# Order of the work in the last stage: first cast of g, w_out in half blocks, banks emptied ahead of g

## Chip, cores and metric

One core of one Trainium2 chip. The metric is the device time of one execution in microseconds (us); a time is the median of several executions.

## The reference

Sliding-window attention with four sink positions, a soft mixture of experts, and a feed-forward block, all in float32. The change lies in the last of the three:

```
x = attention(q, k, v)                     # (3072, 512)
c = softmax(x @ phi, over the slots)       # (3072, 32)
x = c @ slot_out                           # slot_out: (32, 512)
h = x @ w_in                               # (3072, 2048)
g = h - tanh(h)
out = g @ w_out                            # (2048, 512)
```

The host passes `w_out` (and `w_in`) as float64 in 64-bit words; the kernel makes float32 of it itself.

## The kernel before

Every engine's instructions stand in the order in which the program writes them; there is no scheduler. The last stage begins some 235 us into the span. As x is c times a matrix of 32 rows, `x @ w_in` is done as c times (slot_out @ w_in): the "small weights" `W`, 32 rows per 512 columns, are computed by `w_mm` into three PSUM banks (`acc[3]`, `cv_t`, `acc[2]`), and their rows are written to the tiles `w_st[x]` as a high and a low part: `rows_a(x)` casts on ScalarE, `rows_b(x)` subtracts on VectorE (and copies on GpSimd for x = 2). The rest of W goes the same way through `whs_part(x)` (ScalarE) and `wls_part(x)` (VectorE) into `whs` and `wls`, from which `rows4` copies rows later, in steps 5, 11 and 20.

Then come 96 steps. A step s belongs to a chunk c of 512 tokens and to a block f of 128 of the 2048 columns of h. Its parts stand in several steps of the program:

- `hmm(s)` on TensorE: one matmul makes h for chunk and block; it is issued at the end of step s-1.
- `act_y(s)` on ScalarE: tanh of a scaled h in place (L1184), its square into u (L1185). `dve_part(s)` on VectorE: g = u * h (L1204).
- `split(s)`, issued in step s+1: ScalarE casts g to `gh` (L1191), GpSimd subtracts, `gl = g - gh` (L1192).
- `omm(s)`, issued in step s+3: twelve matmuls add gh*whi, gh*wlo and gl*whi to four PSUM banks `acc[0..3]` (tiles o0 to o3; t counts the banks, one for each 128 tokens). In the last step of a group of blocks the three matmuls of a bank stand together, so that bank 0 is done first.
- `evac(s)`, behind the last step of a group: the four banks are copied to SBUF, or added to what is there; after block 15 SyncE issues the output's DMA, one of 128x512 for each bank.

The first chunks don't go through all 16 blocks at once, since `w_out` isn't ready: the groups (chunk, first block, end) are

```python
groups = [(0, 0, 2), (1, 0, 4), (0, 2, 6), (1, 4, 10), (0, 6, 12), (1, 10, 16), (0, 12, 16)] + [(c, 0, 16) for c in range(2, NT // CK)]
```

so `evac` runs in steps 3, 8, 12, 18, 24, 30, 34 and then every 16. Step 4 is the one step without `omm`: it has `hmm(5)` alone.

Ahead of its first use a block f of `w_out` is converted from 64 to 32 bits: `pre_conv` has four VectorE instructions of 128x512, "1" (L108), "2" (L113), "3" (L118), "g" (L127), and a square "s" on ScalarE (L122). Then `wsplit(f)` on GpSimd makes `whi` (L1032) and `wlo` (L1033), and `wload(f + 6)` has SyncE fetch a later block. A block takes two steps: "1" and "2" in the step with ph = 0, "3", "g", `wsplit` and `wload` in the next. `dve_part` puts g behind the first of the VectorE instructions that it is given as `fills`. With `CO = 2`, block f is ready in step 2f-1; `omm` reads block 9 first in step 18 and block 15 first in step 30.

Of the kernel before, what the change touches and what calls it, by code (L numbers as in the profile page):

```python
# [51 lines left out]
WACT = ()  # L52
DL, S0 = 2, 9
CK = 512
CO = 2
SPL = 2
DRAIN = "slota:mi trans slotb av3 av2 av1 d13 d14 d15 pst:sc lg2:sc lg3:sc sink:mi x0:sc,sc max pre exp slots x1:pT,av0 t0 t1 cmax:sc x2:sc,sc trd:sc x3:pT,av0 t2 t3 ext:sc trl:sc csum:sc s00:sc s01 slotc s02 acc0 s10:mi s11 acc1 sT:av0"
XENG = "AAAA"
# [79 lines left out]
def tile_kernel(ctx: ExitStack, tc: tile.TileContext, qk, vv, v0, v0t, nw, phi, w1, w2,  # L138
# [17 lines left out]
    def run(ctx, fast):  # L156
# [30 lines left out]
        for i in range(NR):  # L187
            pool, n = raw_p if i in RAW else ring2 if i in FREE else ring1, 1024 if i in HALF else 2048
# [28 lines left out]
        def ring_t(i, lo, n):  # L217
            if i == NR:
                return xt_t[lo // 512][:, lo % 512:lo % 512 + n]
            if i == NR + 1:  # L220
                return x2[0][:, lo:lo + n]
            return sv(order[i if i < NR else i - NR - 2], lo, n)
# [683 lines left out]
        def raw_of(f):  # L906
            return wraw[(f - 1) % 6]

        def wload(f):
            SP.dma_start(raw_of(f), w_out[P * f:P * f + P, :])  # L910
# [98 lines left out]
        def pre_conv(f, ops):  # L1009
            if f not in pcv:  # L1010
                wf[f] = wf_b[f % 3]
                pcv[f] = conv.start(raw_of(f), wf[f], cv_t if f > 1 else None)
            fns = {"1": conv.v1, "2": conv.v2, "3": conv.v3, "s": conv.sq, "g": conv.guard_dve,
                   "i": conv.ge_pool, "m": conv.mul_pool}
            for o in ops:
                fns[o](pcv[f])
# [10 lines left out]
        def wsplit(f):  # L1027
            hi, lo = whl[f]
            if f in WACT:
                ACT.copy(hi, wf[f])  # L1030
            else:
                POOL.tensor_scalar(hi, wf[f], 1.0, 0.0, op0=ALU.mult, op1=ALU.add)  # L1032
            POOL.tensor_tensor(lo, wf[f], hi.bitcast(F32), op=ALU.subtract)  # L1033
# [15 lines left out]
        for r in range(2):  # L1049
# [17 lines left out]
            for f in range(8):  # L1067
                for g in range(4):
                    t = ring_t(16 + 8 * r + 4 * (f // 4) + g, 512 * (f % 4), 512)
                    PE.matmul(yo[NS * g:NS * g + NS, :], hT[:, f, NS * g:NS * g + NS],  # L1070
                              t, start=f == 0, stop=f == 7)
# [13 lines left out]
            for x in range(2):  # L1085
# [3 lines left out]
                o = 16 * r  # L1089
# [10 lines left out]
        def w_of(f):  # L1100
            x, o = (f, 0) if f < 2 else (2, f - 2) if f < 4 else (2 + f // 4, f % 4)
            return w_st[x][:, P * o:P * o + P]
# [8 lines left out]
        def rows_a(x):  # L1111
            for g in range(2 if x < 2 else 1):
                ACT.copy(w_st[x][NS * g:NS * g + NS, :], W[x][0:NS, :])

        def rows_b(x):
            w = w_st[x]
            hi = w.bitcast(F32)[0:NS, :]
            if x > 1:
                POOL.tensor_scalar(w[NS:2 * NS, :], hi, 1.0, 0.0, op0=ALU.mult, op1=ALU.add)
            DVE.tensor_tensor(w[2 * NS:G3, :], W[x][0:NS, :], hi, op=ALU.subtract)  # L1120
# [3 lines left out]
        steps = [(c, f, f == lo, f == hi - 1) for c, lo, hi in groups for f in range(lo, hi)]  # L1124
        N = len(steps)

        def h_of(s):
            return h_b[s % 2]

        def hmm(s):  # L1130
            c, f = steps[s][:2]
            PE.matmul(h_of(s), w_of(f), cT[0:G3, CK * c:CK * c + CK], start=True, stop=True)  # L1132
# [27 lines left out]
        def whs_part(x):  # L1160
            ACT.copy(whs[:, w_lo[x]:w_lo[x] + w_n[x]], W[x])

        def wls_part(x):
            c = slice(w_lo[x], w_lo[x] + w_n[x])
            DVE.tensor_tensor(wls[:, c], W[x], whs.bitcast(F32)[:, c], op=ALU.subtract)
# [15 lines left out]
        def act_y(s, small=True):  # L1181
            h = h_of(s)
            if small:
                ACT.activation(h, h, AF.Tanh, scale=ca)  # L1184
                ACT.activation(u_b[s % 3], h, AF.Square, scale=cc ** 0.5)  # L1185
            else:
                ACT.activation(u_b[s % 3], h, AF.Square)

        def split(s):
            g, gh, gl = g_b[s % 3], gh_b[s % NG], gl_b[s % NG]  # L1190
            ACT.copy(gh, g)  # L1191
            POOL.tensor_tensor(gl, g, gh.bitcast(F32), op=ALU.subtract)  # L1192

        def dve_part(s, small, fills):
            h, u, g = h_of(s), u_b[s % 3], g_b[s % 3]
            fills = list(fills)

            def fill():
                if fills:
                    fills.pop(0)()  # L1200

            fill()
            if small:
                DVE.tensor_tensor(g, u, h, op=ALU.mult)  # L1204
                fill()
            else:
                DVE.tensor_scalar(mk, u, TB * TB, None, op0=ALU.is_gt)
                DVE.tensor_scalar(z, u, TB * TB, None, op0=ALU.min)
                DVE.tensor_scalar(u, z, cg[6], None, op0=ALU.mult)
                for q in (5, 4, 3, 2, 1, 0):  # L1210
                    DVE.scalar_tensor_tensor(u, u, cg[q], z, op0=ALU.add, op1=ALU.mult)
                fill()
                DVE.tensor_tensor(g, u, h, op=ALU.mult)
                ACT.activation(z, h, AF.Tanh)
                DVE.tensor_tensor(z, h, z, op=ALU.subtract)
                DVE.copy_predicated(g, mk, z)
            while fills:
                fill()

        def omm(s, hi=True, lo=True, ts=range(4)):  # L1220
            c, f, first, last = steps[s]
            gh, gl = gh_b[s % NG], gl_b[s % NG]
            wh, wl = whl[f]

            def mm(t, a, w, start, stop):
                PE.matmul(acc[t], a[:, P * t:P * t + P], w, start=start, stop=stop)  # L1226

            for t in ts:
                if hi:
                    mm(t, gh, wh, first, False)  # L1230
                    mm(t, gh, wl, False, False)
                if last and lo:
                    mm(t, gl, wh, False, True)
            if lo and not last:
                for t in ts:
                    mm(t, gl, wh, False, False)
# [2 lines left out]

        def evac(s):  # L1240
            c, f = steps[s][:2]
            for t in range(4):
                sp = sp_b[c % 2][t]
                if c > 1 or (c, f) in ((0, 1), (1, 3)):
                    if t % 2:
                        DVE.tensor_copy(sp, acc[t])
                    else:
                        ACT.copy(sp, acc[t])
                elif t % 2:
                    ACT.copy(tmp[t], acc[t])  # L1250
                    POOL.tensor_tensor(sp, sp, tmp[t], op=ALU.add)
                else:
                    DVE.tensor_tensor(sp, acc[t], sp, op=ALU.add)
                if f == 15:
                    r0 = CK * c + P * t
                    SP.dma_start(out[r0:r0 + P, :], sp)

        f2 = keep.tile([1, 1], F32, name="f2")
        fmx = h_of(N)[0:1, 0:P]
# [6 lines left out]
        def x_wmax():  # L1266
            ACT.activation(z, whs, AF.Square)
            DVE.tensor_reduce(wmax, z, axis=AX.X, op=ALU.max)
# [3 lines left out]
        def step(s, small, pre=False):  # L1272
            o = s - (DL + 1)
            if pre and s < 5:
                o = 1 if s == 3 else -1
            if o >= 0:
                omm(o)
            if 1 < s + 1 < N:
                hmm(s + 1)
            if fast and s == N:  # L1280
                PE.transpose(fmx, wmax, ident)
            f, ph = divmod(s + CO, 2)
            todo = 2 <= f < 16 and (pre or s >= S0)
            fills = []
            if todo:
                fills = [lambda p=p: pre_conv(f, p) for p in ("3g" if ph else "12")]
            if s < N:
                act_y(s, small)
            if 0 <= s - 1 < N:
                split(s - 1)  # L1290
            if todo and ph == 0:
                pre_conv(f, "s")
            if fast and s == N:
                x_flag()
            if s < N:
                dve_part(s, small, fills)
            if todo and ph:
                wsplit(f)
                if f + 6 < 16:
                    wload(f + 6)  # L1300
            if (pre or s >= S0) and s in row_at:
                rows4(row_at[s])
            if o >= 0 and steps[o][3]:
                evac(o)
            if fast and s == 40:
                x_wmax()

        act_y(0)
        rows_a(1)
# [3 lines left out]
        fq = ctx.enter_context(tc.tile_pool(name="fq", bufs=1))  # L1313
        w_split_tiles(fq, range(NB, 16))
        dve_part(0, True, (lambda: None, lambda: rows_b(1)))
        rows_a(2)
        hmm(1)
        act_y(1)
        split(0)
        rows_b(2)  # L1320
        for x in range(3):
            whs_part(x)
        omm(0, lo=False, ts=(0, 1))
        dve_part(1, True, (lambda: None, lambda: [wls_part(x) for x in range(3)]))
        hmm(2)
        omm(0, lo=False, ts=(2, 3))
        omm(0, hi=False)
# [99 lines left out]
```

## Time and profile before

| | us |
|---|---|
| median of 3 executions | 545.78 (544.48 to 547.65) |
| the profiled execution | 544.87 |
| its span in the trace | 543.1 |
| TensorE busy in the span | 510.2 (94%) |
| mean granted clock of TensorE | 0.993 |

The span is what the trace covers; 1.8 us of the profiled execution lie around it. TensorE is busy nearly all the time, so what matters in the last stage is when it isn't, and at what clock it runs. A matmul lasts longer than the distance to the next one, since they are pipelined: distances between starts are what counts.

### The profile page before, as it was taken

The numbers are of one execution on the slowest core, as the hardware profiler recorded it, in microseconds if no ns is written. First come the engines' busy times: TensorE is split into PE (matmuls) and PEld (weight loads), VectorE is DVE, ScalarE is ACT, GpSimd is POOL, SyncE is SP. The second block draws the span as 40 slices with busy tenths as digits, with TensorE's granted clock in tenths as the row PEclk, the third lists the DMA queues.
The fourth block names the chain that finished last, engine by engine and source line by source line (L and its number), as shares of the span: only waits on it lengthen the run. The fifth ranks groups of instructions, "written<-read, shape, count | busy, mean of one in ns | idle before, by whom it ended". The sixth has DMA issues, their size and how long they took to land.

```text
span 543.1 us, 10098 instructions
## 1 busy us (share of the span) xinstructions
PE 510.2 (94%) x3650; PEld 357.3 (66%) x3650; DVE 314.8 (58%) x672; ACT 356.0 (66%) x1020; POOL 264.4 (49%) x289
## 2 busy tenths in 40 slices
PE   8898999989989998889998998999999999999996
PEld 4555555555555532248776876888888888888884
DVE  2999998998787487667876773322232232223221
ACT  4899898898896333449776765665656565556550
POOL 0566755656734000047897896644343434444441
PEclk9999999999999999999999998999999999999999
DMA  8979886433467899962321002200020020002002
GB/s 307 410 284 346 321 313 226 128 102 121 160 235 248 301 361 410 409 240 77 116 80 40 0 1 77 78 2 0 1 78 1 0 78 0 1 0 78 1 1 82
DMA packets 21993, 77.59 MB, mean 143 GB/s; under 512 B 2866, under 2 KB 4018, under 8 KB 20018
## 3 DMA queue, kind: packets, MB, share of 16 engines
q1 hardware_dynamic: 21938, 76.89, 38.7%
q8 instruction: 30, 0.49, 0.4%
q14 instruction: 25, 0.20, 0.1%
HBM read 70.59 MB, written 6.29 MB: 142 GB/s over the span
## 4 chain that ended last, share of the span: by engine, by line
PE 64%; DVE 12%; DMA 11%; ACT 7%; POOL 3%; issue 2%; SPq 1%; POOLq 0%; DVEq 0%; ACTq 0%
PE o L1226 48%; DMA w<-in_w 7%; PE h L1132 4%; PE av L655 3%; ACT w L591 3%; DVE mx L582 3%; DMA w<-in_qk 2%; DVE w L637 2%; PE sc L561 2%; DMA w<-in_vv 1%; PE mi L427 1%; DVE w L576 1%; PE pT L623 1%; ACT w L575 1%; DVE w L635 1%
## 5 line engine op out<-in xcount | busy, mean ns | idle before, releaser
L1192 POOL TENSOR_TENSOR gl<-g,gh 128x512 fp32r<-128x512 f32 x96 | 123.7, 1290 | 121.3 <-ACT gh L1191 120.4
L1204 DVE TENSOR_TENSOR g<-u,h 128x512 f32<-128x512 f32 x96 | 66.0, 688 | 165.6 <-ACT u L1185 164.9
L1226 PE MATMUL o<-whi,gh 128*128 128x512 f32 x384 | 153.2, 399 | 4.2 <-issue 1.9
L1226 PE MATMUL o<-wlo,gh 128*128 128x512 f32 x384 | 152.5, 397 | 1.7 <-POOL wlo L1033 1.7
L1184 ACT ACTIVATE h<-h 128x512 f32<-128x512 f32 x96 | 55.9, 582 | 98.4 <-PE h L1132 98.2
L1226 PE MATMUL o<-whi,gl 128*128 128x512 f32 x384 | 109.2, 392 | 0.0
L1226 PEld LDWEIGHTS o<-whi,gh 128*128 128x128 f32 x384 | 73.0, 190 | 22.7 <-POOL whi L1032 2.4
L1226 PEld LDWEIGHTS o<-wlo,gh 128*128 128x128 f32 x384 | 73.1, 190 | 19.2 <-POOL wlo L1033 2.3
L1226 PEld LDWEIGHTS o<-whi,gl 128*128 128x128 f32 x384 | 72.7, 189 | 16.3 <-POOL gl L1192 0.6
L601 POOL TENSOR_TENSOR w<-w,su 128x528 f32<-128x528 f32 x38 | 41.3, 1086 | 53.6 <-DVE su L598 34.8
L591 ACT ACTIVATE w<-w,nb 128x132 f32<-128x132 f32 x152 | 59.6, 393 | 1.2
L1185 ACT ACTIVATE u<-h 128x512 f32<-128x512 f32 x96 | 57.3, 597 | 3.0
L1191 ACT CAST gh<-g 128x512 fp32r<-128x512 f32 x96 | 58.9, 614 | 0.4 <-DVE g L1204 0.3
L655 PE MATMUL av<-w,w 128*64 128x256 f32 (+1 forms) x448 | 48.3, 344 | 0.0
L561 PE MATMUL sc<-w 64*64 64x200 f32 (+2 forms) x768 | 45.3, 332 | 1.8 <-DMA w<-in_qk 0.9
L1032 POOL TENSOR_SCALAR whi<-wf 128x512 fp32r<-128x512 f32 x16 | 10.2, 639 | 62.0 <-DMA w<-in_w_out 59.1
L1132 PE MATMUL h<-cT,wst 96*128 96x512 f32 x96 | 38.0, 398 | 0.6 <-DVE wst L1120 0.5
L561 PEld LDWEIGHTS sc<-w 64*64 64x64 f32 x768 | 26.5, 133 | 15.1 <-issue 10.1
L655 PEld LDWEIGHTS av<-w,w 128*64 128x64 f32 x448 | 25.8, 136 | 15.3 <-issue 9.2
L637 DVE TENSOR_TENSOR w<-pT,c_t 128x512 f32<-128x512 f32 x46 | 31.2, 679 | 0.0
L623 PE MATMUL pT<-c_t,w 128*128 128x128 f32 x148 | 23.6, 282 | 6.3 <-POOL w L601 3.8
L591 ACT ACTIVATION_READ_ACCUMULATOR w<-w,nb 128x1 f32 x152 | 28.3, 187 | 0.0
(252 smaller groups left out, 707.7 us busy)
## 6 DMA issues: line engine op xcount, KB each, us to landing
w<-in_w SPq DMA_DIRECT2D x32, 512.0 KB, 10.2
w<-in_w SPq DMA_DIRECT2D x14, 1024.0 KB, 6.7
w<-in_qk SPq DMA_DIRECT2D x16, 780.0 KB, 6.7
w<-in_w_out SPq DMA_DIRECT2D x15, 512.0 KB, 3.6
w<-in_vv SPq DMA_DIRECT2D x16, 384.0 KB, 4.2
w<-in_w_in SPq DMA_DIRECT2D x8, 512.0 KB, 4.8
out<-xt SPq DMA_DIRECT2D x12, 256.0 KB, 2.2
win_t<-in_w_in SPq DMA_DIRECT2D x4, 512.0 KB, 9.6
```

Source lines behind the costliest of these rows:

```text
L561: PE.matmul(sc_t[i][u][w, o:o + n], a[r, 64 * j:64 * j + 64], kslc(a, lo, n)[r, :], start=True, stop=True)
L591: ACT.activation(Z[:, u, :], Z[:, u, :], AF.Exp, bias=nb[:, u:u + 1], scale=SCALE, accum_out=su[:, u, :])
L601: (POOL if i < NQ - 1 else DVE).tensor_tensor(Z, Z, su.to_broadcast([P, 4, CH]), op=ALU.mult)
L637: DVE.tensor_tensor(d[:, :, 0, :], src, mL, op=ALU.mult)
L655: PE.matmul(dst[r, :], v[:, t, r], l, start=start, stop=stop, skip_group_check=True)
L1132: PE.matmul(h_of(s), w_of(f), cT[0:G3, CK * c:CK * c + CK], start=True, stop=True)
L1184: ACT.activation(h, h, AF.Tanh, scale=ca)
L1185: ACT.activation(u_b[s % 3], h, AF.Square, scale=cc ** 0.5)
L1191: ACT.copy(gh, g)
L1192: POOL.tensor_tensor(gl, g, gh.bitcast(F32), op=ALU.subtract)
L1204: DVE.tensor_tensor(g, u, h, op=ALU.mult)
L1226: PE.matmul(acc[t], a[:, P * t:P * t + P], w, start=start, stop=stop)
```

## The change

It has four parts. At the start of the stage the first cast of g (`split(0)`) moves ahead of `hmm(1)`, of tanh and square of step 1 and of the small weights' rows; `whs_part` and `wls_part` move up behind it, `rows_a(2)` behind step 1's tanh and square, and `rows_b(2)` behind step 1's g. A table `plan` gives the half blocks that a step converts: one in two steps of three and two in the third, from step 3 on. `evac` is called ahead of g: its ScalarE copies stand in front of the conversion's square, and its VectorE work is returned as the first `fills` of the step. With that the output's DMAs of a chunk are issued bank 0, bank 2, bank 1, bank 3 (for the chunk whose banks are added up: 1, 3, 0, 2).

```diff
-CO = 2
@@ evac
-            for t in range(4):
+            fresh = c > 1 or (c, f) in ((0, 1), (1, 3))
+
+            def one(t):
                 sp = sp_b[c % 2][t]
-                if c > 1 or (c, f) in ((0, 1), (1, 3)):
+                if fresh:
...
+            dve = [t for t in range(4) if t % 2 == fresh]
+            for t in range(4):
+                if t not in dve:
+                    one(t)
+            return [lambda t=t: one(t) for t in dve]
@@ step
-            f, ph = divmod(s + CO, 2)
-            todo = 2 <= f < 16 and (pre or s >= S0)
+            todo = plan.get(s, ()) if pre or s >= S0 else ()
...
+            if o >= 0 and steps[o][3]:
+                fills += evac(o)
+            for f, ph in todo:
+                fills += [lambda f=f, p=p: pre_conv(f, p) for p in ("3g" if ph else "12")]
+                if not ph:
+                    pre_conv(f, "s")
...
-            if o >= 0 and steps[o][3]:
-                evac(o)
...
+        turns = [(2, 1)] + [(f, ph) for f in range(3, 16) for ph in range(2)]
+        plan, s_ = {}, 3
+        while turns:
+            n = 2 if s_ % 3 == 1 else 1
+            plan[s_], turns = turns[:n], turns[n:]
+            s_ += 1
@@ ahead of the steps
         dve_part(0, True, (lambda: None, lambda: rows_b(1)))
+        split(0)
+        hmm(1)
+        for x in (0, 2, 1):
+            whs_part(x)
+            wls_part(x)
+        act_y(1)
         rows_a(2)
-        hmm(1)
-        act_y(1)
-        split(0)
-        rows_b(2)
-        for x in range(3):
-            whs_part(x)
         omm(0, lo=False, ts=(0, 1))
-        dve_part(1, True, (lambda: None, lambda: [wls_part(x) for x in range(3)]))
+        dve_part(1, True, (lambda: None, lambda: rows_b(2)))
         hmm(2)
         omm(0, lo=False, ts=(2, 3))
```

Lines below L57 have a number smaller by one in the changed kernel, and by other amounts below `evac`. The first place is ScalarE at the start of the stage. Before, the rows from the casts of the small weights to the third tanh (h is tanh in place, u the square, gh the cast of g, whs the rest of the small weights) are:

```order
L1113 CAST wst1_3234<-cvt_2878 32x128 x2
L1113 CAST wst2_3235<-o2_2875 32x256
L1184 ACTIVATE h1_2872<-h1_2872 128x512
L1185 ACTIVATE u1_3299<-h1_2872 128x512
L1191 CAST gh0_3301<-g0_3295 128x512
L1161 CAST whs_3293<-o3_2876 128x128
L1161 CAST whs_3293<-cvt_2878 128x128
L1161 CAST whs_3293<-o2_2875 128x256
L1184 ACTIVATE h0_2871<-h0_2871 128x512
```

In the changed kernel the same stretch is:

```order
L1112 CAST wst1_3234<-cvt_2878 32x128 x2
L1190 CAST gh0_3301<-g0_3295 128x512
L1160 CAST whs_3293<-o3_2876 128x128
L1160 CAST whs_3293<-o2_2875 128x256
L1160 CAST whs_3293<-cvt_2878 128x128
L1183 ACTIVATE h1_2872<-h1_2872 128x512
L1184 ACTIVATE u1_3299<-h1_2872 128x512
L1112 CAST wst2_3235<-o2_2875 32x256
L1183 ACTIVATE h0_2871<-h0_2871 128x512
```

The cast of g moved up over the cast into wst2 and step 1's tanh and square, the three casts into whs went with it, and the cast into wst2, which reads bank o2, now stands behind step 1's square.

The second place is VectorE in the same stretch, from the first g to the first conversion of block 2. Before:

```order
L1204 TENSOR_TENSOR g0_3295<-u0_3298,h0_2871 128x512
L1120 TENSOR_TENSOR wst1_3234<-cvt_2878,wst1_3234 32x128
L1120 TENSOR_TENSOR wst2_3235<-o2_2875,wst2_3235 32x256
L1204 TENSOR_TENSOR g1_3296<-u1_3299,h1_2872 128x512
L1165 TENSOR_TENSOR wls_3294<-o3_2876,whs_3293 128x128
L1165 TENSOR_TENSOR wls_3294<-cvt_2878,whs_3293 128x128
L1165 TENSOR_TENSOR wls_3294<-o2_2875,whs_3293 128x256
```

In the changed kernel:

```order
L1203 TENSOR_TENSOR g0_3295<-u0_3298,h0_2871 128x512
L1119 TENSOR_TENSOR wst1_3234<-cvt_2878,wst1_3234 32x128
L1164 TENSOR_TENSOR wls_3294<-o3_2876,whs_3293 128x128
L1164 TENSOR_TENSOR wls_3294<-o2_2875,whs_3293 128x256
L1164 TENSOR_TENSOR wls_3294<-cvt_2878,whs_3293 128x128
L1203 TENSOR_TENSOR g1_3296<-u1_3299,h1_2872 128x512
L1119 TENSOR_TENSOR wst2_3235<-o2_2875,wst2_3235 32x256
```

The last reader of bank o2 was the third subtraction into wls; now it is the subtraction into wst2, behind the second g.

The third place is VectorE in steps 3 to 5 (g0 to g2 take turns; xt1 and xt3 are banks copied out; cvt and wf belong to the conversion). Before:

```order
L1204 TENSOR_TENSOR g0_3295<-u0_3298,h1_2872 128x512
L127 SCALAR_TENSOR_TENSOR wf2_3099<-cv_3100,cvt_2878 128x512
L1246 COPY xt1_136<-o1_2874 128x512
L1246 COPY xt3_138<-o3_2876 128x512
L108 TENSOR_SCALAR cvt_2878<-w3_0_117 128x512
L1204 TENSOR_TENSOR g1_3296<-u1_3299,h0_2871 128x512
L113 SCALAR_TENSOR_TENSOR cvt_2878<-w3_0_117,cvt_2878 128x512
L118 SCALAR_TENSOR_TENSOR cvt_2878<-w3_0_117,cvt_2878 128x512
L1204 TENSOR_TENSOR g2_3297<-u2_3300,h1_2872 128x512
```

In the changed kernel:

```order
L1247 COPY xt1_136<-o1_2874 128x512
L1203 TENSOR_TENSOR g0_3295<-u0_3298,h1_2872 128x512
L1247 COPY xt3_138<-o3_2876 128x512
L117 SCALAR_TENSOR_TENSOR cvt_2878<-w2_0_116,cvt_2878 128x512
L126 SCALAR_TENSOR_TENSOR wf2_3099<-cv_3100,cvt_2878 128x512
L107 TENSOR_SCALAR cvt_2878<-w3_0_117 128x512
L1203 TENSOR_TENSOR g1_3296<-u1_3299,h0_2871 128x512
L112 SCALAR_TENSOR_TENSOR cvt_2878<-w3_0_117,cvt_2878 128x512
L117 SCALAR_TENSOR_TENSOR cvt_2878<-w3_0_117,cvt_2878 128x512
L126 SCALAR_TENSOR_TENSOR wf0_3097<-lg_71,cvt_2878 128x512
L107 TENSOR_SCALAR cvt_2878<-w3_0_117 128x512
L1203 TENSOR_TENSOR g2_3297<-u2_3300,h1_2872 128x512
```

The copies stand in front of and behind step 3's g, and between the g of step 4 and that of step 5 there are now four instructions of conversion where there were two.

## Rows read from the trace of the kernel before

**Rows 1.** Stretches: us; busy PE, PEld, DVE, ACT, POOL; granted clock; DMA; GB/s.

```profile
240.00:246.00 6.00, 4.16 (x11) 3.34 (x12) 3.98 (x9) 4.33 (x10) 1.99 (x4) 0.72 0.04 16
...
330.00:336.00 6.00, 5.26 (x16) 4.22 (x17) 2.02 (x3) 1.80 (x4) 3.39 (x4) 0.72 0.14 53
```

**Rows 2.** Chain of work that ended last, late in the stage: start, length.

```profile
445.87 0.23 PE h L1132
...
448.86 0.23 PE h L1132
```

**Rows 3.** TensorE in order of time, start of the stage: start, length, idle before.

```profile
239.49 0.50 PE L1132 MATMUL h<-cT,wst 96*128 96x512 f32 x1
241.84 0.47 PE L1226 MATMUL o<-whi,gh 128*128 128x512 f32 x1 [1.85 <-issue]
242.14 0.48 PE L1226 MATMUL o<-wlo,gh 128*128 128x512 f32 x1
242.41 0.63 PE L1226 MATMUL o<-whi,gh 128*128 128x512 f32 x1
...
246.48 0.39 PE L1132 MATMUL h<-cT,wst 96*128 96x512 f32 x1
```

**Rows 4.** TensorE in order of time, at later waits.

```profile
273.92 0.39 PE L1132 MATMUL h<-cT,wst 96*128 96x512 f32 x1
274.70 0.47 PE L1226 MATMUL o<-whi,gh 128*128 128x512 f32 x1 [0.39 <-DVE xt L1253]
...
289.49 0.39 PE L1132 MATMUL h<-cT,wst 96*128 96x512 f32 x1
290.65 0.50 PE L1226 MATMUL o<-whi,gh 128*128 128x512 f32 x1 [0.77 <-POOL whi L1032]
292.01 0.50 PE L1226 MATMUL o<-wlo,gh 128*128 128x512 f32 x1 [0.86 <-POOL wlo L1033]
...
331.07 0.63 PE L1226 MATMUL o<-whi,gl 128*128 128x512 f32 x1
...
334.94 0.39 PE L1132 MATMUL h<-cT,wst 96*128 96x512 f32 x1
```

**Rows 5.** ScalarE and VectorE in order of time, start of the stage.

```profile
238.43 0.69 DVE L1204 TENSOR_TENSOR g<-u,h 128x512 f32<-128x512 f32 x1 [0.38 <-DMA w<-in_w_out]
...
239.91 0.41 DVE L1120 TENSOR_TENSOR wst<-o,wst 32x256 fp32r<-32x256 f32 x1 [0.48 <-ACT wst L1113]
240.02 0.58 ACT L1184 ACTIVATE h<-h 128x512 f32<-128x512 f32 x1
240.63 0.60 ACT L1185 ACTIVATE u<-h 128x512 f32<-128x512 f32 x1
241.13 0.61 ACT L1191 CAST gh<-g 128x512 fp32r<-128x512 f32 x1
...
241.95 0.40 ACT L1161 CAST whs<-o 128x256 fp32r<-128x256 f32 x1
```

**Rows 6.** VectorE by group, 246 to 330 us: count, busy, mean ns.

```profile
L118 DVE SCALAR_TENSOR_TENSOR cvt<-w,cvt 128x512 uint32<-128x512 uint32 x14 | 9.7, 692 | 0.3
```

**Rows 7.** GpSimd by group, 246 to 330 us.

```profile
L1192 POOL TENSOR_TENSOR gl<-g,gh 128x512 fp32r<-128x512 f32 x28 | 36.2, 1293 | 12.8 <-ACT gh L1191 11.9 <-POOL wst L1158 0.6
L1033 POOL TENSOR_TENSOR wlo<-wf,whi 128x512 fp32r<-128x512 f32 x14 | 18.1, 1296 | 1.2
L1032 POOL TENSOR_SCALAR whi<-wf 128x512 fp32r<-128x512 f32 x14 | 9.0, 642 | 0.0
```

**Rows 8.** Line 1156 by itself, the copies of rows4: ns min/median/max.

```profile
L1156 DVE CAST wst<-wls x3: 746/751/1236, 254.8 to 300.7; 32x512 fp32r<-32x512 f32 x3
```

**Rows 9.** SyncE in order of time, end of the program: start, length of issue.

```profile
536.61 1.12 SPq L1256 DMA_DIRECT2D out<-h  x2
537.97 0.33 SPq L1256 DMA_DIRECT2D out<-v_t  x1
```

**Rows 10.** GB/s moved by DMA in 40 slices of 535 to 545 us.

```profile
GB/s 0 0 66 0 0 0 0 0 0 74 385 377 230 377 352 385 385 369 377 410 369 99 57 16 33 0 0 0 0 0 0 0 0 0 0 0 0 0 0 0
```

More of the change, by code (lines that the diff above doesn't have):

```diff
@@ L1281, in step @@
                 PE.transpose(fmx, wmax, ident)
-            f, ph = divmod(s + CO, 2)
-            todo = 2 <= f < 16 and (pre or s >= S0)
+            todo = plan.get(s, ()) if pre or s >= S0 else ()
             fills = []
-            if todo:
-                fills = [lambda p=p: pre_conv(f, p) for p in ("3g" if ph else "12")]
             if s < N:
@@ L1290, in step @@
                 split(s - 1)
-            if todo and ph == 0:
-                pre_conv(f, "s")
+            if o >= 0 and steps[o][3]:
[4 more added lines that the diff above has]
+                    pre_conv(f, "s")
             if fast and s == N:
@@ L1296, in step @@
                 dve_part(s, small, fills)
[L1297 to L1300, printed above, removed]
+            else:
+                for fn in fills:
+                    fn()
+            for f, ph in todo:
+                if ph:
+                    wsplit(f)
+                    if f + 6 < 16:
+                        wload(f + 6)
             if (pre or s >= S0) and s in row_at:
                 rows4(row_at[s])
-            if o >= 0 and steps[o][3]:
-                evac(o)
             if fast and s == 40:
                 x_wmax()
+        turns = [(2, 1)] + [(f, ph) for f in range(3, 16) for ph in range(2)]
[4 more added lines that the diff above has]
+            s_ += 1
         act_y(0)
```

## Prediction

> **What bounds the kernel now.** I read the chain of waits first. From the start of the last stage to the end TensorE stands in it, and late in the stage a step takes 448.86 - 445.87 = 2.99 us for 13 matmuls, 0.23 us each, with no gap [rows 2]. That work isn't touched. What can be won is the time by which the earlier steps exceed it, so I went through TensorE's instructions in order of time and added up, over every distance between starts that is longer than 0.23, the excess.
>
> At the start, 2.12 us lie between the h matmul of step 1 (239.49) and the first `omm` matmul (241.84), which waits for the cast of g, started only at 241.13 [rows 3, 5]. The first distances behind a wait are longer as well: 242.14 - 241.84 = 0.31, so 0.08 more, and 0.04 in the next. From 242.41 to 246.48 there are 11 distances that should take 2.53 and take 4.07, an excess of 1.54: the granted clock of this stretch is 0.72, a mixture of 1.2 and 2.4 GHz [rows 1, 3]. At 273.92 the bank to be overwritten is still being emptied by VectorE: 0.55, with the 0.08 behind it 0.63; the same occurs once more some 39 us later, 1.26 for both [rows 4]. At 289.49 TensorE waits for whi and then wlo of block 9: 2.52 to the start of the wlo matmul, of which 0.46 is work; 2.06, with 0.1 behind it 2.16 [rows 4]. Block 15 does the same some 39 us later, so 4.3 for both. Behind that second one the clock falls again: 331.07 to 334.94 are ten distances, 3.87 in place of 2.30, excess 1.57 [rows 1, 4].
>
> Sum of the excess: 2.24 + 1.54 + 1.26 + 4.3 + 1.57 = 10.9 us.
>
> **The cast of g first.** g of step 0 ends at 238.43 + 0.69 = 239.12 [rows 5]. In the new order nothing else stands before its cast on ScalarE then, so it starts at about 239.15, 1.98 earlier than 241.13, and the first `omm` matmul comes at 241.84 - 1.98 = 239.86. Of 2.24 some 0.2 stay.
>
> But the order shows a wait that takes its place. The matmuls of bank 2 overwrite the bank from which `rows_b(2)` reads, and that subtraction now stands behind step 1's g on VectorE, behind tanh and square on ScalarE. Worked forward from the new start: cast of g to the last `whs` cast 241.95 - 241.13 = 0.82, that one 0.3, so tanh at 240.27; square 0.61 later, done 0.60 after it, 241.48; g 0.69 on VectorE (the next starts 0.6 after it), 242.1 to 242.15; `rows_b(2)` 0.41, done at about 242.55 [rows 5]. TensorE is through the four matmuls of banks 0 and 1 and the h matmul of step 2 at 239.86 + 5 * 0.23 = 241.0. It waits 1.6, with what is behind a wait 1.7. Queued behind that on TensorE is everything. Bounds: 1.2 if the subtraction comes up against nothing else, 2.2 if it also waits behind the conversion's first instruction (0.69 [rows 6]). I take 1.7, as the chain has no free place.
>
> **The clock.** Both falls come behind waits: 1.85 us at one time, 0.77 and 0.86 at the other; but the same 0.77 and 0.86 at 290.65 and 292.01 were followed by full speed [rows 3, 4]. So 1.6 us of waiting is followed by 1.2 GHz in some executions and not in others, and the new wait of 1.6 has about the chance of one in three. I take none as the likeliest, and 1.5 as the price. The Trainium skill (TensorE: Matmul & The Clock Gate, "HAM oscillation") has an abstract rule by which only gaps longer than any of these lower the clock. By it neither fall would be, and the gain would be smaller by 3.1; the trace shows both, so the measurement decides.
>
> **Half blocks.** Block 9 is now ready in step 13 (used in 18), block 15 in step 22 (used in 30), so both waits go, 4.3, and with them the second fall of the clock, 1.57. What pays is VectorE and GpSimd. In steps 3 to 5 VectorE has four instructions of conversion between the g of step 4 and that of step 5 where there were two, and step 4 gives TensorE only one matmul. Two copies of banks, two g and six of conversion are ten instructions of 0.69 [rows 6], 6.9 us, while TensorE has 3.2 us in steps 3 and 4 and 2.99 in step 5. VectorE reaches bank 3 only when step 3's matmuls end. Laid out instruction by instruction as above, its g of steps 4 and 5 end some 0.4 and 0.3 after the time at which TensorE wants to overwrite their h. With that the subtraction into gl of step 5 is 0.2 late, and the copies of banks 1 and 3 in step 8, now behind two instructions of conversion, 0.1 and 0.2. Five short waits of 1.25 and 0.08 behind each: 1.7. Bounds: none, as before (VectorE caused no wait here), and 3.0, if one more 0.69 stands in each of the two long ones.
>
> GpSimd has 14 blocks of 0.642 + 1.296, 20 gl of 1.293, and three copies and two additions that I put at the same 0.64 and 1.29, in steps 3 to 22: 57.5 us [rows 7], against 19 * 2.99 + 0.23 = 57.1 for TensorE. It is exactly full. What saves it is distance: gl of a step is made about 3.4 us into the next step (0.4 until tanh, 0.61, 0.50, 0.61 and 1.29 [rows 5, 7]) and read at the earliest 0.5 us into the step two behind that, 2 * 2.99 - 3.4 + 0.5 = 3.1 us later, 4.5 in most steps. I charge 0.3. Bounds: 0, and 2.5, if GpSimd is late by that much more than its room. One thing delays it for certain: a copy on VectorE that normally takes 0.75 took 1.24 when GpSimd was at work [rows 8], and there are three of them.
>
> The Trainium skill (SBUF — State Buffer, "SBUF: two separate sides") has VectorE and GpSimd exclude each other for a whole instruction where VectorE reads two SBUF tensors or uses both its ports for one. Here each converting instruction and each g has an operand in PSUM, so by it only the three copies matter; the 1.24 agrees. It speaks for the 0.3 and against rival 3.
>
> The loads of w_out are issued at each block's end, six blocks, so nine steps or 27 us, ahead of their conversion; I charge nothing for them. The squares on ScalarE stand behind the bank copies and have a step to spare.
>
> **Banks ahead of g.** In step 12 the addition of bank 0 now starts when the bank is done, some 0.9 us into the step, not behind g and two conversions; it ends before the next step's first matmul. Both waits of 0.63 go: 1.26. g is put off by less than 0.7 there, and it is read three steps later. At the end of the program, however, SyncE now issues banks in the order 0, 2, 1, 3. The DMA engines moved the last four outputs in one unbroken stretch from 537.4 to 540.3, so 0.7 us each [rows 10]; issue began at 536.61 [rows 9]. Bank 0 is moved by 538.1, and bank 2, issued at 537.97, starts 0.8 after its issue, at 538.8, while bank 1 waits behind it. The end comes at 538.8 + 3 * 0.7 = 540.9: 0.5 later. Bounds 0 and 0.7.
>
> **Sum.** Gone: 10.9. New: 0.2 + 1.7 + 1.7 + 0.3 + 0.5 = 4.4. Net 6.5, so the profiled execution's 544.87 becomes 538.4. The median before stands 0.9 above that execution, well inside the spread of its three runs, and I take the same distance for the changed kernel: 545.78 - 6.5 = **539.3 us**.
>
> **The rivals.** (1) The clock falls behind the new wait: 1.5 more, 540.8. For: 1.85 of waiting did it. Against: one of two waits of 1.63 didn't. (2) GpSimd or VectorE is late by its bound: 2.5 - 0.3 and 3.0 - 1.7 more, 542.8 at the end, 541 in the middle. For: GpSimd is full. Against: instructions of one kind differ by hundredths. (3) The other side: GpSimd becomes the bound of steps 3 to 22. To be 0.5% slower, it has to eat 6.5 + 2.7 and its room of 3.1, 12.3 us in 53 instructions, so 0.23 on each; from there each further 0.1 adds 5.3, and at 0.23 the time is 548.5. Against: its mean is 1.29 in a stretch where VectorE is as dense [rows 6, 7]. (4) The change doesn't do what it says, because the blocks of w_out are late for the earlier conversion: both waits stay, 539.3 + 4.3 + 1.6 = 545.2. Against: a block is asked for 27 us before its conversion.
>
> **How the numbers follow.** Forecast (no fall, short waits as worked out) 0.50, rival 1 0.25, rival 2 0.15, rival 4 0.05, rival 3 0.05. The range reaches down by the bounds of VectorE's and GpSimd's terms (1.7 and 0.3) and by the 0.5 of the wait for bank 2 to 536.8, and up to rival 2 at 542.8. A difference of 0.5% (2.7 us) is about what a measurement can tell from no change. Faster by more holds for the forecast, rival 1 and most of rival 2: 0.85. Slower is rival 3 with a little more: 0.05. The rest is 0.10.
>
> **What would show it.** The first `omm` matmul at 239.9, then a wait of about 1.6 us for VectorE's wst ahead of bank 2; no wait for whi or wlo; no wait at 274 and 313; short waits for g, for gl and for a copied bank between 250 and 264; a granted clock of 1.00 behind 246; a GpSimd that is busy nearly all the time to 305; at the end bank 2's output issued before bank 1's, with a dip in GB/s. Wrong it would be if waits for gl appear in steps 12 to 22 (then rival 2 or 3), or if the clock falls in more places than one.

## Result and the profile after

The changed kernel takes **539.53 us** (median of 6 executions, 538.06 to 540.76); the kernel before, executed beside it, 545.45 (6, 544.21 to 547.65). The ratio is 0.9888, 95% interval 0.9861 to 0.9915: 1.1% faster, and the interval doesn't reach 1. The profiled execution took 540.22, its span is 538.4, the mean granted clock 0.993.

The stretches that [rows 1] show of before, and one between them: us; busy PE, PEld, DVE, ACT, POOL; granted clock; DMA; GB/s.

```profile
240.00:246.00 6.00, 4.53 (x31) 2.87 (x24) 4.67 (x10) 4.80 (x12) 4.18 (x5) 1.00 0.20 79
246.00:250.00 4.00, 4.00 (x19) 3.17 (x18) 2.17 (x4) 3.28 (x7) 1.38 (x2) 1.00 0.00 0
330.00:336.00 6.00, 6.00 (x27) 4.90 (x27) 1.37 (x2) 3.65 (x8) 4.92 (x4) 1.00 0.46 175
```

Where 0.72 stood, 1.00 stands, in both places. That the mean clock is 0.993 as before lies ahead of the stage, where the clock of this execution fell behind a wait of 1.91 for a load:

```profile
212.00:216.00 4.00, 3.18 (x11) 0.69 (x12) 1.64 (x3) 0.00 (x0) 0.00 (x0) 0.72 1.03 410
```

TensorE in order of time at the start of the stage, which answers to [rows 3] (start, length, idle before):

```profile
240.78 0.49 PE L1131 MATMUL h<-cT,wst 96*128 96x512 f32 x1
241.16 0.47 PE L1225 MATMUL o<-whi,gh 128*128 128x512 f32 x1
241.47 0.40 PE L1225 MATMUL o<-wlo,gh 128*128 128x512 f32 x1
...
242.17 0.40 PE L1131 MATMUL h<-cT,wst 96*128 96x512 f32 x1
244.01 0.49 PE L1225 MATMUL o<-whi,gh 128*128 128x512 f32 x1 [1.44 <-DVE wst L1119]
244.34 0.39 PE L1225 MATMUL o<-wlo,gh 128*128 128x512 f32 x1
```

The first `omm` matmul now stands 0.38 behind the h matmul, where it stood 2.35. Then bank 2 waits for the subtraction into wst: 244.01 - 242.17 = 1.84 in place of 0.23, so 1.6 (the idle time in brackets is counted from the modelled end of the matmul before, and is smaller). All that TensorE waits for from 239 us on, by line and releaser (us in total, times, longest):

```profile
PE o L1225 <- DVE wst L1119: 1.4, 1, 1.4
PE o L1225 <- POOL gl L1191: 0.6, 2, 0.4
PE h L1131 <- DVE g L1203: 0.2, 1, 0.2
```

No wait for whi, for wlo or for a bank that is being emptied is left of those in [rows 4]. The short ones in order of time:

```profile
252.51 0.50 PE L1131 MATMUL h<-cT,wst 96*128 96x512 f32 x1
...
255.95 0.50 PE L1131 MATMUL h<-cT,wst 96*128 96x512 f32 x1 [0.20 <-DVE g L1203]
...
260.24 0.50 PE L1225 MATMUL o<-whi,gl 128*128 128x512 f32 x1 [0.18 <-POOL gl L1191]
...
308.99 0.50 PE L1225 MATMUL o<-whi,gl 128*128 128x512 f32 x1 [0.39 <-POOL gl L1191]
```

As excess over 0.23 between starts they are 0.30, 0.35, 0.34 and 0.56, each with 0.11 behind it. Late in the stage nothing changed; the chain as in [rows 2], a step of 2.99:

```profile
443.26 0.23 PE h L1131
446.25 0.23 PE h L1131
```

GpSimd and VectorE by group, 246 to 330 us, for [rows 6, 7] (count, busy, mean ns, idle before):

```profile
L1191 POOL TENSOR_TENSOR gl<-g,gh 128x512 fp32r<-128x512 f32 x29 | 37.7, 1308 | 9.8 <-ACT gh L1190 9.6
L1032 POOL TENSOR_TENSOR wlo<-wf,whi 128x512 fp32r<-128x512 f32 x14 | 18.1, 1296 | 1.2
L1031 POOL TENSOR_SCALAR whi<-wf 128x512 fp32r<-128x512 f32 x14 | 8.8, 632 | 1.9 <-DVE wf L126 1.9
L117 DVE SCALAR_TENSOR_TENSOR cvt<-w,cvt 128x512 uint32<-128x512 uint32 x14 | 9.7, 694 | 0.4
```

Only gl became longer in the mean (1.293, 1.296, 0.642 and 0.692 before). Of the copies of [rows 8] none takes 1.24 now, and the shortest shows that 0.42 is enough for one:

```profile
L1155 DVE CAST wst<-wls x3: 420/477/852, 256.5 to 299.7; 32x512 fp32r<-32x512 f32 x3
```

It is GpSimd that now loses time beside them: its instructions at the three places took 1.49, 1.48 and 0.81 where their kinds take 1.29, 1.29 and 0.63, so 0.57 in all (GpSimd in order of time):

```profile
256.62 1.49 POOL L1191 TENSOR_TENSOR gl<-g,gh 128x512 fp32r<-128x512 f32 x1
...
273.04 1.48 POOL L1191 TENSOR_TENSOR gl<-g,gh 128x512 fp32r<-128x512 f32 x1
...
300.20 0.81 POOL L1031 TENSOR_SCALAR whi<-wf 128x512 fp32r<-128x512 f32 x1
```

The end of the program: SyncE's issues (start, length), then GB/s in 40 slices of 529 to 539 us, for [rows 9, 10].

```profile
531.00 0.33 SPq L1257 DMA_DIRECT2D out<-h  x1
532.36 0.33 SPq L1257 DMA_DIRECT2D out<-v_t  x1
532.78 0.38 SPq L1257 DMA_DIRECT2D out<-h  x1
533.26 0.40 SPq L1257 DMA_DIRECT2D out<-c_t  x1
```

```profile
GB/s 33 0 0 0 66 0 0 0 0 0 0 238 377 377 66 25 66 385 369 369 418 369 352 401 344 58 33 33 49 0 0 0 0 0 0 0 0 0 0 0
```

Bank 0 is moved by 532.5, then the engines stand at 25 to 66 GB/s for some 0.75 us. From the last issue to the end of the span it is 538.4 - 533.26 = 5.14, where it was 543.1 - 538.75 = 4.35; the last issue before:

```profile
538.75 0.33 SPq L1256 DMA_DIRECT2D out<-c_t  x1
```

For what follows one measure is used that leaves out what happens ahead of the stage: the time from the h matmul of step 1 to the end of the span, in each profiled execution. It is 543.1 - 239.49 = **303.6** before and 538.4 - 240.78 = **297.6** after, 6.0 less. (In the profiled times the difference is only 4.65, because this execution reached the h matmul 1.3 later; the last section comes to that.)

### The profile page after: what moved, and what is told of

Same layout as the page of the kernel before. It is cut to its first block, busy times and chain, and to the rows that moved or that the text cites. A ratio compares the mean times of both kernels' runs of the same rounds, so it can differ in the third digit from the quotient of the medians.

```text
span 538.4 us, 10099 instructions
## 1 busy us (share of the span) xinstructions
PE 506.7 (94%) x3650; PEld 354.4 (66%) x3650; DVE 314.6 (58%) x672; ACT 356.2 (66%) x1020; POOL 264.4 (49%) x289
## 4 chain that ended last, share of the span: by engine, by line
PE 63%; DVE 12%; ACT 8%; DMA 7%; POOL 5%; issue 2%; SPq 1%; POOLq 0%; ACTq 0%
PE o L1225 44%; DMA w<-in_w 4%; PE h L1131 4%; PE av L654 3%; ACT w L590 3%; DVE mx L581 3%; DMA w<-in_qk 2%; POOL gl L1191 2%; DVE w L636 2%; PE sc L560 2%; DMA w<-in_vv 1%; PE cvt L1069 1%; PE mi L426 1%; DVE w L575 1%; PE pT L622 1%
## 5 line engine op out<-in xcount | busy, mean ns | idle before, releaser
L1225 PE MATMUL o<-whi,gh 128*128 128x512 f32 x384 | 151.6, 395 | 1.4 <-DVE wst L1119 1.4
L1225 PE MATMUL o<-wlo,gh 128*128 128x512 f32 x384 | 150.9, 393 | 0.0
```

## Experiments

| kernel | median, us | before beside it | ratio, 95% interval | stage, us |
|---|---|---|---|---|
| changed kernel | 539.53 | 545.45 | 0.9888 [0.9861, 0.9915] | 297.6 |
| start alone | 542.53 | 544.92 | 0.9953 [0.9933, 0.9974] | 301.8 |
| half blocks alone | 539.68 | 544.92 | 0.9907 [0.9880, 0.9934] | 299.0 |
| banks alone | 544.46 | 544.92 | 0.9995 [0.9971, 1.0019] | 304.2 |
| outputs in order | 537.74 | 544.92 | 0.9867 [0.9840, 0.9894] | 296.7 |
| banks behind g again | 539.30 | 545.05 | 0.9903 [0.9877, 0.9929] | 299.5 |
| wlo twice | 544.13 | 545.05 | 0.9986 [0.9973, 0.9999] | 303.1 |
| rows of bank 2 first | 538.23 | 545.05 | 0.9876 [0.9855, 0.9896] | 297.7 |
| one half block in step 4 | 537.65 | 545.05 | 0.9866 [0.9844, 0.9887] | 296.6 |
| wait filled, before | 542.84 | 544.20 | 0.9980 [0.9962, 0.9998] | 301.4 |
| two casts on ScalarE | 538.59 | 544.20 | 0.9889 [0.9870, 0.9909] | 297.0 |
| both edits | 536.57 | 544.20 | 0.9856 [0.9833, 0.9879] | 295.6 |
| both, wait filled | 536.94 | 544.20 | 0.9853 [0.9830, 0.9876] | 295.6 |

"Stage" is the measure above, of the one profiled execution of each kernel. It is the sharper of the two: a median holds what the clock did in its executions, a stage can be gone through wait by wait. Two kernels that are the same up to the last matmul (changed, outputs in order) both have 291.2 from the h matmul of step 1 to its start. The intervals of most ratios near 0.99 overlap: by the medians the half blocks alone can't be told from the whole change. What is said below of less than 2 us rests on the stages, one execution each.

### The three parts, one at a time

**The start alone**: the kernel before with the diff's last hunk.

```diff
+        split(0)
+        hmm(1)
...
-        dve_part(1, True, (lambda: None, lambda: [wls_part(x) for x in range(3)]))
+        dve_part(1, True, (lambda: None, lambda: rows_b(2)))
```

> The kernel before with only the start of the changed one (first cast of g ahead, rows and whs/wls in the new order); half blocks and banks as before. By the sum of the prediction the start's 2.24 go, 0.2 and 1.7 come: about 0.4 us less, and up to 1.9 less if the 1.54 of the clock's fall go too (the start then has a wait of 1.6 in front of bank 2 where it had 1.85 in front of the first omm matmul). The waits for whi and wlo of blocks 9 and 15 (2.06 each), the second fall of the clock and the two bank waits (0.55) stay. The rival, that the start is worth most of the gain, expects 4 us or more less here.

Measured: 2.4 us less in the median, 1.8 less in the stage. The 2.24 went and bank 2 waits 1.6; in the profiled execution one fall of the clock is left of two:

```profile
240.00:246.00 6.00, 4.56 (x20) 3.38 (x20) 4.21 (x8) 4.74 (x11) 2.72 (x3) 1.00 0.02 6
288.00:294.00 6.00, 4.71 (x13) 3.54 (x14) 3.31 (x6) 2.61 (x6) 4.19 (x4) 0.75 0.02 5
330.00:336.00 6.00, 5.95 (x26) 4.88 (x27) 2.07 (x3) 2.77 (x5) 4.65 (x5) 1.00 0.39 146
```

It is the theory's upper end: 0.3 by the waits, 1.5 by the clock. The waits for whi and wlo of blocks 9 and 15 are the same as before, but now the clock falls behind those of block 9 and not behind those of block 15.

**The half blocks alone**: the kernel before with the table `plan`, evac behind g as it was.

```diff
-            f, ph = divmod(s + CO, 2)
-            todo = 2 <= f < 16 and (pre or s >= S0)
+            todo = plan.get(s, ()) if pre or s >= S0 else ()
...
+            n = 2 if s_ % 3 == 1 else 1
+            plan[s_], turns = turns[:n], turns[n:]
...
```

> The kernel before with only the table of half blocks; evac stays behind g, the start is the old one. Theory: the two waits for whi and wlo go (4.3), with them the second fall of the clock (1.57); the start's 2.24 and its clock's fall and the bank waits in steps 12 and 18 or 24 stay, and step 8, whose bank copies now stand behind four instructions of conversion, gets a bank wait of up to 2 us; short waits for h and gl as in the changed kernel, 1 us. Net 2 to 4 us less. The rival, that the half blocks need the banks ahead of g to be of any use, expects no gain: new bank waits of 4 us or more.

Measured: 5.2 us less in the median, 4.6 in the stage. All waits for whi and wlo are gone; the expected bank wait in step 8 is there, and a wait for gl of step 1, in step 3, that wasn't expected:

```profile
245.65 0.50 PE L1226 MATMUL o<-whi,gl 128*128 128x512 f32 x1 [0.68 <-POOL gl L1192]
...
263.07 0.50 PE L1226 MATMUL o<-whi,gh 128*128 128x512 f32 x1 [1.49 <-DVE h L1246]
```

The clock didn't fall anywhere in the stage (1.00 in 240 to 246, behind the same wait of 1.85 as before), which made the gain larger than expected. The half blocks are of use without the banks; that rival is out.

**The banks alone**: the kernel before with evac ahead of g, one half block a step. The cut is against the changed kernel, whose start is put back to the old one as well.

```diff
...
+        plan = {s_: [divmod(s_ + 2, 2)] for s_ in range(3, 30)}
...
```

> The kernel before with only the banks emptied ahead of g; start and half blocks as before. Theory: the two bank waits at 274 and 313 go (1.26), short waits of some 0.4 each for h and gl come in steps 5 and 8, and the tail is 0.5 to 0.8 longer, since outputs are issued 0, 2, 1, 3: net within 0.5 us of the kernel before. The rival, that the banks alone bring a measurable part of the gain, expects 1.5 us or more less.

Measured: no change (0.9995), the stage 0.6 longer. Both bank waits went (1.26); in their place 0.31 ahead of the h matmul issued in step 5 and 0.56 for gl in step 8, with what is behind them, and a tail from the last matmul to the end of 6.4 in place of 5.5. As the theory had it.

By the stage the three parts add up: -1.8 - 4.6 + 0.6 = -5.8, and the changed kernel has -6.0. In part that is chance: the fall of the clock at the start, 1.54, is gone in the first two of these executions and so counted twice, while the half blocks alone pay for a bank wait of 1.65 and a wait for gl of 0.84 that the changed kernel doesn't have.

### The banks within the changed kernel, and the outputs' order

**Banks behind g again**: the changed kernel with the old place of `evac`.

```diff
...
-            if o >= 0 and steps[o][3]:
-                fills += evac(o)
...
+            if o >= 0 and steps[o][3]:
+                evac(o)
```

> The changed kernel with evac back behind g and the conversion, so the new start and the table of half blocks alone. Theory: the bank waits come back, one in step 8 behind four instructions of conversion (1.65 where the half blocks alone were run) and two of 0.55, with what is behind a wait 3.0; the tail loses 0.8 and the waits for h in steps 4 and 5 some 0.9, the wait for gl in step 24 some 0.67: 0.6 to 1.3 us more than the changed kernel, 540.1 to 540.8. The rival, by the times of the kernels with one part each (2.4 and 5.2 us less): both together without the banks are as fast as the changed kernel or faster, 538.5 or less.

Measured: 539.30, a ratio of 0.9903 against 0.9888; neither expectation is met by the median. The stage has 299.5, but the clock fell in this execution, behind the wait for bank 2 (TensorE in order of time, and the stretch with its granted clock behind the busy times):

```profile
243.64 0.68 PE L1226 MATMUL o<-whi,gh 128*128 128x512 f32 x1 [1.44 <-DVE wst L1120]
244.11 0.63 PE L1226 MATMUL o<-wlo,gh 128*128 128x512 f32 x1
244.54 0.63 PE L1226 MATMUL o<-whi,gh 128*128 128x512 f32 x1
```

```profile
243.00:247.00 4.00, 3.36 (x8) 2.70 (x9) 3.14 (x6) 1.82 (x4) 1.50 (x2) 0.60 0.00 0
```

Eight distances of 0.43 in place of 0.23 are 1.6; without them 297.9, 0.3 more than the changed kernel. The bank waits came back as expected (1.64 and twice 0.55, with what is behind them 3.0). But 2.6 left: the tail 0.8, two waits for h 0.87, that for gl in step 24 0.67, and two small ones of 0.1. So by the traces banks ahead of g are worth 0.3 to 0.4 here, which the medians don't show: the outputs' order and the waits that they bring take the rest.

**Outputs in order**: the changed kernel with the DMAs issued behind the step's copies, bank 0, 1, 2, 3.

```diff
+            def put():
+                for t in range(4 if f == 15 else 0):
...
+            if o >= 0 and steps[o][3]:
+                put()
```

> The changed kernel with the output's DMAs issued behind the step's copies in the order bank 0, 1, 2, 3. Theory: the dip in GB/s at the end goes, and the time from the last issue to the end of the span falls from 5.1 us to the 4.35 of the kernel before: 0.5 to 0.8 us less in all. The rival, that the last output's landing is set by its own length and the end of the matmuls, expects no change (0.1 us).

Measured: 296.7, 0.9 less than the changed kernel; the ratio went from 0.9888 to 0.9867. SyncE's last issue, and GB/s in 40 slices of 527 to 537 us:

```profile
531.16 0.33 SPq L1259 DMA_DIRECT2D out<-c_t  x1
```

```profile
GB/s 33 0 0 66 0 0 0 0 0 33 0 221 369 369 238 377 393 361 369 377 377 401 311 33 57 8 33 0 0 0 0 0 0 0 0 0 0 0 0 0
```

The dip is gone, and from the last issue to the end it is 535.5 - 531.16 = 4.34 again. By the trace the theory holds and the rival is out; the two ratios alone lie too close to show it.

### GpSimd's full time

**wlo twice** for blocks 8 to 11 in the changed kernel:

```diff
-            POOL.tensor_tensor(lo, wf[f], hi.bitcast(F32), op=ALU.subtract)
+            for _ in range(2 if 8 <= f < 12 else 1):
+                POOL.tensor_tensor(lo, wf[f], hi.bitcast(F32), op=ALU.subtract)
```

> The changed kernel with the subtraction into wlo done twice for blocks 8 to 11: 4 more instructions of 1.26, 5.0 us of work for GpSimd in steps 11 to 16, result unchanged. Theory: GpSimd works without a gap from 258 us on and its room is used up by step 24 (a wait of 0.56 there), so TensorE is late by 4 to 5 us, in waits for gl in steps 14 to 24. The prediction's room of 3.1 would leave 1.9 us. The rival, that GpSimd's full time doesn't matter, expects under 1 us.

Measured: stage 303.1, 5.5 more for 5.0 us of work, above what either expected; the rest is the longer distances behind the waits. All of it arrives as waits for gl (TensorE's waits from 239 us on):

```profile
PE o L1226 <- POOL gl L1192: 4.5, 6, 1.3
PE o L1226 <- DVE wst L1120: 1.4, 1, 1.4
PE h L1132 <- DVE g L1204: 0.4, 2, 0.2
```

The first that the changed kernel doesn't have, 0.93 and 0.11 behind it, stands in step 15, when only block 8's 1.26 has been added. So GpSimd's room there is some 0.2 to 0.3: nearly all that it gets more, the kernel takes longer. The prediction's room of 3.1 is refuted. It took gl to be made right behind its gh; in the changed kernel gl stands in GpSimd's queue behind whi and wlo, by 3.8 us for the one that step 24 waits for (ScalarE and GpSimd in order of time):

```profile
303.25 0.61 ACT L1190 CAST gh<-g 128x512 fp32r<-128x512 f32 x1
...
307.66 1.28 POOL L1191 TENSOR_TENSOR gl<-g,gh 128x512 fp32r<-128x512 f32 x1
```

**Two casts on ScalarE** take work away from GpSimd (`WACT` names the blocks whose cast into whi ScalarE makes):

```diff
-WACT = ()
+WACT = (10, 12)
```

> The changed kernel with the cast into whi of blocks 10 and 12 on ScalarE in place of GpSimd, 0.7 us less for GpSimd in each. Theory: the wait for gl in step 24 (0.56 and 0.11 behind it) is GpSimd's fullness and goes, 0.5 to 0.7 us less. The rival: ScalarE, whose instructions stand in order, waits for the end of the conversion with tanh, square and cast of g queued behind it, and TensorE waits for gh or h in steps 15 to 19, 0.5 us or more in place of what is gained.

Measured: 297.0, 0.6 less; the wait for gl in step 24 is gone, and ScalarE causes none. The ratio, 0.9889, doesn't show it; a difference of 0.1% is smaller than the interval. By the trace the theory holds.

### Where the new waits can and can't be moved

**Rows of bank 2 first**, the changed kernel with:

```diff
+        rows_a(2)
         act_y(1)
-        rows_a(2)
...
-        dve_part(1, True, (lambda: None, lambda: rows_b(2)))
+        dve_part(1, True, (lambda: rows_b(2),))
```

> The changed kernel with the cast and the subtraction of the third small weight's rows ahead of step 1's tanh, square and g. Theory: nothing is won, the wait moves: bank 2 from 1.6 to some 0.6, but tanh, g and gl of step 1 are 0.8 later and TensorE waits for gl instead; 0.3 us less at most. The rival, that the wait for bank 2 is only a matter of where rows_b(2) stands, expects 1.0 us less.

Measured: 297.7 against 297.6. The wait for bank 2 fell from 1.6 to 0.46, and gl of step 1 is late by 0.86:

```profile
240.99 0.50 PE L1225 MATMUL o<-whi,gh 128*128 128x512 f32 x1 [0.29 <-DVE wst L1119]
...
244.70 0.50 PE L1225 MATMUL o<-whi,gl 128*128 128x512 f32 x1 [0.70 <-POOL gl L1191]
```

The wait moved, as the theory had it. The start is a chain, not a matter of one instruction's place.

**One half block in step 4**, the changed kernel with:

```diff
-            n = 2 if s_ % 3 == 1 else 1
+            n = 2 if s_ > 5 and s_ % 3 == 1 else 1
```

> The changed kernel with one half block in step 4 in place of two (the first double step is 7). Theory: the four instructions of conversion between the g of steps 4 and 5 are what makes h and gl late between 250 and 264 us; with two, at least the wait for h of step 5 (0.35 and 0.11 behind it) and one of the others go, 0.5 to 0.8 us less. The rival, that the bank copies ahead of g make these waits by themselves (they stood in the kernel with the banks alone too), expects less than 0.3 us of change.

Measured: 296.6, 1.0 less. The wait for h at 255.95 is gone, the one at 252.51 stays (0.33), that for gl of step 8 grew from 0.34 to 0.57; the wait for gl in step 24 is gone as well, which wasn't expected. Four instructions of conversion between two g caused one of the long waits; the first comes from the copies of step 3, as in the kernel with the banks alone. Each theory had half.

**Both edits** (outputs in order, one half block in step 4):

> The changed kernel with the output's DMAs in bank order and one half block in step 4. If both gains add up (0.8 and 1.0 by the traces): 1.8 us less than the changed kernel, a ratio to the kernel before of 0.984 to 0.986. If the tail hides one of them: 0.987.

Measured: 536.57, ratio 0.9856, stage 295.6, 2.0 less than the changed kernel: they add up. Together with the last kernel below (both, wait filled) it is the fastest version found.

### The clock

**Wait filled, before**: the kernel before with

```diff
         hmm(1)
+        for _ in range(7):
+            PE.matmul(acc[0], w_of(0), cT[0:G3, 0:CK], start=True, stop=True)
```

> The kernel before with seven more matmuls behind the h matmul of step 1, into bank 0, which the first omm matmul overwrites (result unchanged): 1.6 us of work in the wait of 1.85 for the cast of g. Theory: the clock falls because TensorE stood idle there; without the idle time the granted clock of the first 6 us behind it is 1.00, the eleven distances are 0.23 and not 0.43, while the first omm matmul comes at the same time. The median falls by 0.5 to 1.5 us, by the share of the executions in which the clock falls. The rival, that the fall has nothing to do with the wait, expects a fall as before and no change of the median.

Measured: 1.4 us less in the median (0.9980, its interval just below 1), 2.2 in the stage. The mean granted clock was 0.996 or more in 9 of 12 executions, in 5 of 17 of the kernel before beside them, so falls became rarer; the profiled execution alone wouldn't show that, since one of three with the wait unfilled had no fall there either. The first `omm` matmul comes as late as before (2.35 behind the h matmul), the clock stays at 1.00, but one wait is new:

```profile
241.76 0.47 PE L1226 MATMUL o<-whi,gh 128*128 128x512 f32 x1 [0.21 <-issue]
...
246.39 0.50 PE L1226 MATMUL o<-whi,gl 128*128 128x512 f32 x1 [0.70 <-POOL gl L1192]
```

It is the wait for gl of step 1 that the half blocks alone had too: at 1.2 GHz TensorE was slow enough to hide it. So a fall at the start costs 1.54 by its distances and, in the old order, 1.54 - 0.86 - 0.1 = 0.6 in the end. The second fall is absent from this execution too, which gives the rest: 1.54 + 1.57 - 0.96 = 2.15.

**Both edits, wait filled**: six more matmuls into bank 3 during the new wait.

```diff
         hmm(2)
+        for _ in range(6):
+            PE.matmul(acc[3], w_of(0), cT[0:G3, 0:CK], start=True, stop=True)
```

> The kernel with both edits (outputs in bank order, one half block in step 4) and six more matmuls into bank 3 during the wait for bank 2, which bank 3's first omm matmul overwrites (result unchanged). Theory: the wait of 1.6 lets the clock fall in some executions, as it did in the one with evac back behind g (243.8); filled, it never does, so the median falls by 0.1 to 0.5 us and the slowest execution by up to 1.5. The rival: matmuls that do nothing make others late, or the falls come elsewhere; no change or 0.2 more.

Measured: 0.9853 and 295.6 against 0.9856 and 295.6, slowest executions 537.33 and 537.32. No difference; with four executions each, a fall in one of eight would hardly be seen.

## Why the prediction was right

539.3 was forecast and 539.53 measured. The sum, term by term, with the excess over 0.23 read from the trace after:

- **Gone, 10.9**: all five terms went. (Of the start, 2.35 lie between the h matmul and the first `omm` matmul; the 2.12 of the prediction is the excess.) The 0.2 that was to stay of the start is 0.15, with 0.08 behind it 0.23.
- **Bank 2, 1.7**: 1.6 and 0.1. The chain worked forward from the casts held to 0.1: from the start of the cast of g to the end of the subtraction it is 3.51 (240.44 to 243.95), where 3.40 was worked out. Its place, behind step 1's g, held too.
- **Short waits, 1.7**: 1.6 in all. The two for h are 0.30 and 0.35, where 0.4 and 0.3 were forecast; gl of step 5, read in step 8, was 0.34 late, where it was 0.2. The copied banks of step 8 cost 0.04 at most, not 0.1 and 0.2; 0.06 ahead of step 5's first `omm` matmul and 0.10 for gl of step 4 weren't foreseen. What is behind the waits makes up the rest.
- **GpSimd, 0.3**: mis-sized. 0.56 and 0.11 in step 24, 0.67. The step that failed is the room of 3.1 us: doubling wlo shows next to none, since gl waits in GpSimd's full queue behind its gh. The delay named for certain was there, on the other engine: no copy took over 0.85, but GpSimd lost 0.57 beside them, and from 254.67 on it has no gap over 0.1 in which to make that up. By these rows that loss is as long as the wait; no run takes it away by itself. The 0.75 that the prediction calls normal for a copy already held a delay, since 0.42 is enough.
- **Tail, 0.5**: mis-sized, 0.8 by the last issue and the end, shown by putting the issue back in order. (By the prediction's own times, 540.3 and 540.9, it was 0.6.) The mechanism, bank 1 waiting behind bank 2, holds.
- **The clock**: of eight profiled executions with the new wait of 1.6, one had a fall behind it. Rival 1 so exists; eight are too few to tell its chance from one in three. What the sum left out is that the fall at the start had covered a wait for gl; it cost nothing here, since the new start makes gh and gl of step 1 early enough.

New in all, as measured: 0.23 + 1.7 + 1.6 + 0.67 + 0.8 = 5.0. 10.9 - 5.0 = 5.9, which is the difference of the medians (545.45 - 539.53) and of the stages (6.0); the prediction had 6.5, from a median of before that lay 0.3 higher. So of the 0.6 by which the new waits were put too low, half was made up by that median: that the time came out within 0.2 is in part luck.

Rival 2 was partly there, within its bounds. Rival 3 is nearer than it looked: not by slower instructions, but because GpSimd is already the second bound of this stretch. Rival 4 didn't happen: no conversion waits for a load.

## What to carry to other kernels

Add up the excess of the bounding engine's distances between starts, wait by wait, and then ask for each wait that goes what is late next: here five went for 10.9, and 5.0 came back, most of it at places that were named beforehand. Here an engine that was full over a stretch passed on all that it was given; double a piece of its work to see that. And when the order of copies is changed, look at the order of the DMAs that follow them: 0.8 us lay there, twice the 0.3 to 0.4 that the copies' new place was worth in all.

## What the runs showed of the hardware

- **The clock falls behind some waits, and not behind others of the same length.** The waits for whi and wlo of block 9 (0.77 and 0.86) were followed by 1.2 GHz with the start alone and the banks alone, and not before; those of block 15 before, and not in these two. The wait of 1.85 at the start was followed by a fall in two of three executions, 1.6 in front of bank 2 in one of eight. Ahead of the stage one of 1.91 for a load was followed by a fall in the execution after, one of 1.92 at the same place in the kernel with the banks behind g again wasn't. What decides it these runs don't show. It is a part of the spread of the kernel before: its two executions with a mean clock of 1.00 took 542.0 and 542.95, its medians are 544.2 to 545.8; but those with one and the same clock of 0.993 still took 543.2 to 545.79.
- **VectorE can be held up while GpSimd works.** In the profiled execution after, ahead of the stage (VectorE and GpSimd in order of time):

```profile
235.71 1.32 POOL L1032 TENSOR_TENSOR wlo<-wf,whi 128x512 fp32r<-128x512 f32 x1
...
235.94 1.64 DVE L112 SCALAR_TENSOR_TENSOR wf<-w,wf 128x512 uint32<-128x512 uint32 x1
...
237.92 0.69 DVE L117 SCALAR_TENSOR_TENSOR wf<-w,wf 128x512 uint32<-128x512 uint32 x1
```

An instruction with both its operands in SBUF took 1.64 beside wlo, and the next of its kind 0.69 without it. That is the exclusion that the Trainium skill (SBUF — State Buffer, "SBUF: two separate sides") states, and the 1.64 agrees. The reverse stands among the rows above, the gl of 1.49 and 1.48 beside a copy. Of the 1.3 us by which this execution reached the h matmul of step 1 later, 1.0 arose here: from VectorE's copy into so just ahead (234.38 before, 234.70 after) to the h matmul it is 5.11 before and 6.08 after. The other 0.3 was there already. In the fourteen profiled executions the h matmul stood at 238.67 to 240.78 and that copy at 233.19 to 234.95, so most of this spread comes from further ahead, from a place where the program is still the same; its cause isn't shown.
